# Another written-out order of all engines' steps for the first half of a fused attention and gated-MLP kernel

## The chip, the cores and the metric

The kernel runs on one core of a Trainium2 chip. The core has a matrix engine (PE, with its weight loads shown apart as PEld), a vector engine (DVE), a scalar engine (ACT), a general engine (POOL) and a queue that issues the transfers from and to HBM (SP). Each works through its own queue of instructions strictly in the order in which they were written, and waits at an instruction until what it needs is there. The metric is the time of one execution on the device in microseconds (us); lower is better.

## What is computed

Eight batches of windowed attention with eight heads, 576 positions and 64 numbers per head, and behind it a gated MLP with a spatial gate over the 576 positions (the reference, cut):

```python
scores = scale * np.matmul(q, k.transpose(0, 1, 3, 2))          # q, k, v: (8, 8, 576, 64)
mask = (rel >= 0) & (rel < 128)
scores = np.where(mask, scores + bias[None], -1000000000.0)
attn = np.exp(scores - np.max(scores, axis=-1, keepdims=True))
attn = attn / (np.sum(attn, axis=-1, keepdims=True) + 1e-09)
x = np.matmul(attn, v)                                          # then (8, 576, 512)

h = gelu(x @ w_in)                                              # w_in: (512, 1024)
u, v = h[..., :512], h[..., 512:]
v_n = (v - mu) / np.sqrt(var + 1e-06) * g_ln
v_s = np.einsum('ts,bsd->btd', w_sg, v_n) + b_sg[None, :, None] # w_sg: (576, 576)
out = x + (u * v_s) @ w_out                                     # w_out: (512, 512)
```

## The kernel before

The work is cut into steps, each a closure that issues a few instructions on one engine. A step's name is a letter or two and a number. Attention goes by pairs of heads: 32 pairs, numbered 0 to 31, four to a batch. The MLP goes by batch, 0 to 7. All matrix products of the MLP are made of three products of high and low halves, so everything that goes into them is split into a high part (ACT) and a low part (POOL or DVE).

The steps of pair n (`Pair.STEPS`), in the order of their needs:

- SP: q loads query and key, L loads the values (six transfers).
- PE: a and c are the scores of the first and second half of the positions for pairs 0 to 4; * is both at once for the later pairs.
- DVE: A, B, C, G add the bias and find the maxima of four score banks (lines 273 and 266). ACT: e, E, f, F, j are the exponentials. DVE: R inverts the sums (lines 294 and 295). POOL: r, s, S scale.
- PE: z, t, T transpose; DVE: X, Y copy the transposed weights out under a mask (line 318); ACT: P copies the first block.
- PE: 2 and v (for later pairs 3 and V) multiply with the values (lines 329 and 342). ACT: x gathers the result (lines 350 and 351), h takes its high part (line 356), POOL: l its low part (line 359), ACT: k a copy of the last columns (line 362).

The weights are split at the start, a tile k at a time: SP i loads; ACT d; DVE m, b, o (lines 183, 185, 187); POOL +; ACT H; then the low part -, on POOL for even k and on DVE for odd k (line 194). Tiles 0 to 7 are w_in, of which 4 to 7 are needed by u, and 8 to 11 are w_out. The spatial weights go by wl, wH, w- (SP, ACT, POOL); tl, tH, t- and bl, bH, b- are their tail and the bias; gb loads the gain. The loads of all these share a ring of four buffers, so a load waits until the step that last read its buffer is done: w-, + and so on.

The steps of batch b's MLP:

- PE: v, per block of 128 positions (in batch 0 in four parts, w and v); ACT: vg; DVE: nv..b and nv..c, POOL: nv..p, ACT: nv..h, DVE: vn normalize it.
- The same for the last 64 positions: PE tt; DVE tj; ACT tg; DVE nt..b and nt..c (lines 579 to 587); POOL nt..p; ACT nt..h; DVE tn (line 595, into vA).
- PE: u, eight sums to a batch (lines 559 to 561 with `xs` first); ACT: uc, ug.
- PE: y, eight spatial sums (the same lines with `ws`), whose last two matmuls alone read what tn wrote; DVE gm, ACT gh, POOL gl gate and split.
- PE: O, the output sums (Oa is the first three quarters of the first one); DVE oa adds, SP D stores.

A step y020 is batch 0, column block 2, half 0; nv30b is block 3 of batch 0.

What sets the order is a string, `ORDER`, with all step names. A small planner checks that each step comes after what it needs and that buffers are free, and runs the steps in that order. A manual dependency then keeps each engine's instructions in the order of the string. So the string is each engine's queue; steps of different engines that stand side by side in it need not run side by side.

```python
for run in plan.run(ORDER.split()):
    before = len(nc.cur_bb.bb.instructions)
    run()
    for i in nc.cur_bb.bb.instructions[before:]:
        if i.engine in last:
            tc.add_manual_dep(i, last[i.engine], ...)
        last[i.engine] = i.name
```

Of the kernel before, what the change touches and what calls it, by code (L numbers as in the profile page):

```python
# [21 lines left out]
def attention_gmlp(  # L22
# [754 lines left out]
    for b in range(B):  # L777
# [7 lines left out]
        T2 l1 q5 d6 G3 z2 +4 Y2 a4 F3 L3 P2 j3 -2 A4 22 v2 k1 H4 m6 e4 R3 -4 B4 i3 w21 x2 o5 c4 b6 h2 L5 r3 w11 j4 s3 C4
        w31 E4 G4 S3 t3 f4 w01 X3 F4 l2 i10 T3 d3 z3 Y3 +5 w12 q6 P3 k2 R4 *5 o6 H5 m3 i11 -5 b3 w22 A5 s4 q7 w32 +6 e5
        B5 23 w02 v3 j5 o3 i8 C5 S4 E5 H6 G5 +3 L4 x3 f5 r4 t4 -6 h3 T4 X4 d11 l3 i9 z4 Y4 H3 d8 -3 m11 k3 v03 P4 m8 F5
        b11 24 v01 b8 R5 v4 o11 vg03 o8 vg01 s5 nv30b v02 x4 r5 v00 nv30c nv10b nv30p t5 z5 S5 d9 X5 +11 nv30h T5 P5 +8
        d10 Y5 nv10p H11 35 m10 H8 V5 vn03 -11 vg00 nv10c u000 nv00b -8 L6 x5 nv10h b10 *6 vn01 nv00c vg02 L7 o10 u001 A6
        +10 nv20b u010 nv00p uc00 B6 q8 nv20p nv00h nv20c H10 u011 vn00 nv20h bl m9 C6 -10 tt0 uc01 G6 vn02 u020 bH b9  # L790
        tj0 u021 o9 tg0 b- u030 nt0b +9 uc02 nt0c H9 u031 nt0p -9 nt0h *7 uc03 tn0 ug0 y000 q9 A7 B7 h5 y020 h4 l5 C7 G7
        y001 l4 j6 k5 F6 y021 k4 E6 gm00 f6 e6 y010 gm02 E7 R6 s6 j7 y011 gh00 S6 f7 gh02 gl00 y030 gm01 e7 gh01 r6 gl02
        F7 z6 t6 y031 P6 X6 gl01 R7 T6 s7 gm03 Oa0 Y6 gh03 S7 gl03 *8 r7 O02 q10 A8 e8 B8 E8 C8 O00 j8 G8 f8 36 z7 oa00
        t7 V6 P7 oa02 F8 D00 D02 R8 s8 T7 L9 x6 X7 O03 S8 h6 Y7 l6 r8 37 k6 oa03 V7 D03 O01 L8 x7 h7 l7 *9 oa01 k7 D01
# [10 lines left out]
        S14 oa10 v23 Y13 r14 D10 vg22 nv22b t14 vg23 nv22c u230 x12 nv22p nv32b nv22h 313 nv32c V13 vn22 nv32p u231 L15
        x13 X14 nv32h *15 uc23 vn23 ug2 L14 y210 A15 h13 B15 h12 z14 l13 y220 q17 P14 C15 l12 G15 k13 T14 y211 Y14 e15
        E15 *16 gm21 F15 f15 y200 gh21 q19 A16 j15 gl21 B16 e16 y221 E16 C16 R15 f16 G16 y201 s15 gm22 F16 S15 gh22 t15
        gm20 j16 y230 gl22 gh20 R16 k12 gl20 314 y231 r16 s16 V14 gm23 S16 gh23 r15 Oa2 gl23 x14 X15 h14 l14 T15 O23 Y15
        k14 z15 t16 oa23 P15 O20 D23 315 T16 oa20 V15 D20 O21 L16 x15 X16 h15 Y16 l15 L17 *17 oa21 k15 u300 A17 q18 e17
        B17 v30 j17 C17 D21 f17 G17 E17 z16 u301 F17 P16 R17 v31 uc30 s17 S17 vg30 r17 nv03b t17 vg31 316 tt3 nv03c nv13b  # L810
        nv03p V16 nv03h nv13c vn30 u330 nv13p L19 x16 X17 nv13h z17 u331 vn31 P17 tj3 *19 uc33 tg3 nt3b O22 q21 A19 nt3p
        B19 nt3c e19 v32 C19 nt3h oa22 G19 D22 f19 tn3 j19 v33 E19 F19 R19 u320 r19 s19 vg32 vg33 nv23b T17 S19 u310
        nv33b nv23p nv33c u321 Y17 nv33p nv33h u311 nv23c uc32 vn33 nv23h *18 uc31 vn32 h16 ug3 l16 y320 q20 A18 B18 k16
        y300 C18 e18 G18 y321 E18 f18 j18 y301 gm32 F18 gh32 R18 y330 gl32 gm30 gh30 s18 317 y310 S18 gl30 t19 y311 r18
        z19 y331 gm31 P19 gh31 gl31 V17 gm33 gh33 Oa3 gl33 L18 x17 X19 h17 l17 T19 O32 Y19 k17 z18 t18 oa32 P18 319 O30
        D32 V19 oa30 D30 T18 L20 x19 X18 O33 h19 Y18 l19 k19 318 oa33 V18 D33 O31 L21 x18 h18 l18 *20 oa31 k18 D31 u400
        A20 e20 B20 tt4 j20 C20 f20 G20 u401 tj4 E20 F20 *21 uc40 R20 s20 u430 q22 A21 r20 tg4 S20 B21 t20 q23 v40 C21
        e21 nt4b E21 j21 nt4c u431 f21 G21 nt4p nt4h X20 T20 v41 F21 tn4 uc43 Y20 R21 v42 vg40 r21 s21 vg41 nv04b S21
        nv14b nv04p v43 nv14c nv04c nv14p nv04h nv14h vn40 z20 u420 vn41 vg42 P20 vg43 nv24b *22 nv34b nv24p nv34c u410
        q24 A22 nv34p nv34h u421 B22 C22 u411 e22 nv24c j22 G22 f22 z21 320 t21 vn43 V20 nv24h uc42 vn42 E22 y400 F22 L23  # L820
        X21 P21 x20 R22 T21 s22 h20 y401 Y21 uc41 r22 S22 *23 l20 ug4 y420 q25 A23 k20 gm40 B23 t22 gh40 y410 gl40 C23
        G23 e23 321 y421 E23 j23 z22 f23 V21 gm42 F23 P22 gh42 R23 y430 L22 X22 x21 s23 h21 S23 T22 y411 Y22 r23 l21 *24
        gl42 gm41 k21 gh41 y431 gl41 q27 A24 e24 B24 Oa4 E24 C24 gm43 f24 G24 gh43 322 z23 t23 F24 V22 gl43 P23 j24 R24
        T23 x22 X23 O43 r24 s24 h22 Y23 S24 l22 323 O40 oa43 V23 k22 D43 oa40 D40 O41 L24 x23 h23 l23 L25 *25 oa41 k23
# [53 lines left out]
```

## Time and profile before

| | us |
|---|---|
| median of 3 runs | 641.43 |
| the runs | 641.43, 639.53, 645.07 |
| profiled execution, first to last instruction (its span) | 639.6 |
| PE busy, share of the span | 606.7, 95% |
| DVE busy | 385.3, 60% |
| ACT busy | 356.2, 56% |
| POOL busy | 236.7, 37% |

The profile comes from one execution; it has the span, and of the whole time of that execution nothing beyond it, so the median of the runs stands beside it: 641.43 to 639.6. Busy is the time in which an engine executes. A row with min/median/max gives the length of one instruction in ns. In the rows in order of time the first two numbers are start and length in us, and a bracket at the end tells how long the engine was idle before and who ended that.

### The profile page before, as it was taken

The page shows a single profiled execution, that of the slowest core. Times are in us where ns is not written, and L with a number is a line of the kernel's source. Part 1 is how long each engine was busy: PE and PEld are TensorE (multiplying, and loading weights), DVE is VectorE, ACT ScalarE, POOL GpSimd, SP SyncE. Part 2 cuts the span into 40 slices and gives each one's busy share as a digit, 9 for nine tenths or more (in the row PEclk, how much of TensorE's full clock was granted, in tenths as well). Part 3 has the DMA queues.
Part 4 walks back from the last instruction along what each step waited for, and adds up shares of the span by engine and source line. Part 5 has one row for each costly group of instructions (what it writes and reads, how often), then busy time and mean ns, then how long its engine had stood idle before and what let it go on. Part 6 is the DMA issues. An engine that isn't in the chain of part 4 may idle for free.

```text
span 639.6 us, 14817 instructions
## 1 busy us (share of the span) xinstructions
PE 606.7 (95%) x5664; PEld 552.6 (86%) x5664; DVE 385.3 (60%) x1297; ACT 356.2 (56%) x1045; POOL 236.7 (37%) x237
## 2 busy tenths in 40 slices
PE   4877789999999999999999999999999999999997
PEld 2555579898999898998999989998999989999896
DVE  5899788445854587545753577547664465452611
ACT  8784756645582676725672478647483455543430
POOL 4776633632244323632233142542235222441220
PEclk9999699999999999999999999999999999999999
DMA  8875331051132413223311512224122321110001
GB/s 277 261 214 180 107 116 38 1 172 57 40 114 70 141 38 104 71 78 98 93 38 58 173 38 76 79 95 115 40 93 73 103 94 40 40 39 38 0 1 75
DMA packets 55931, 57.24 MB, mean 89 GB/s; under 512 B 8498, under 2 KB 45362, under 8 KB 55860
## 3 DMA queue, kind: packets, MB, share of 16 engines
q1 hardware_dynamic: 55860, 56.28, 28.3%
q8 instruction: 45, 0.74, 0.5%
q14 instruction: 26, 0.21, 0.1%
HBM read 46.83 MB, written 9.44 MB: 88 GB/s over the span
## 4 chain that ended last, share of the span: by engine, by line
PE 84%; DVE 8%; ACT 2%; issue 2%; POOL 1%; DMA 1%; SPq 0%; POOLq 0%; DVEq 0%
PE ps_m L559 20%; PE ps_m L561 19%; PE ps_m L560 19%; PE ps_s L342 7%; PE ps_s L247 4%; PE ps_a L309 4%; PE ps_a L247 3%; DVE e L266 2%; DVE px L318 2%; PE ps_a L342 1%; PE ps_m L707 1%; PE ps_m L706 1%; DVE tmp L187 1%; PE ps_m L643 1%; PE ps_m L645 1%
## 5 line engine op out<-in xcount | busy, mean ns | idle before, releaser
L282 ACT ACTIVATE e<-e,stats 128x128 f32<-128x128 f32 (+1 forms) x320 | 121.1, 380 | 33.8 <-DVE stats L266 32.5
L299 POOL TENSOR_TENSOR e<-e,rr 128x512 f32<-128x512 f32 (+1 forms) x96 | 79.9, 853 | 130.4 <-DVE rr L295 103.0
L559 PE MATMUL ps_m<-ws,vn 128*128 128x288 f32 x256 | 79.1, 309 | 0.0
L559 PE MATMUL ps_m<-g,wo 128*128 128x288 f32 x256 | 78.8, 308 | 0.0
L559 PE MATMUL ps_m<-xs,wi 128*128 128x288 f32 x256 | 78.4, 306 | 0.1
L561 PE MATMUL ps_m<-g,wo 128*128 128x288 f32 x256 | 75.9, 296 | 0.0
L561 PE MATMUL ps_m<-xs,wi 128*128 128x288 f32 x256 | 75.7, 296 | 0.0
L561 PE MATMUL ps_m<-ws,vn 128*128 128x288 f32 x256 | 75.7, 296 | 0.0
L560 PE MATMUL ps_m<-xs,wi 128*128 128x288 f32 x256 | 75.6, 295 | 0.0
L560 PE MATMUL ps_m<-ws,vn 128*128 128x288 f32 x256 | 75.6, 295 | 0.0
L560 PE MATMUL ps_m<-g,wo 128*128 128x288 f32 x256 | 75.0, 293 | 0.5 <-POOL g L719 0.5
L359 POOL TENSOR_TENSOR xs<-xf,xs 128x576 fp32r<-128x576 f32 x32 | 45.8, 1432 | 77.8 <-ACT xs L356 77.6
L318 DVE TENSOR_TENSOR px<-ps_a,m_old 128x512 f32<-128x512 f32 x64 | 43.9, 687 | 49.5 <-PE ps_a L309 37.0
L584 POOL TENSOR_TENSOR rs<-rs,mhalf 128x1 f32<-128x1 f32 (+1 forms) x40 | 32.6, 814 | 96.7 <-DVE rs L581 90.1
L719 POOL TENSOR_TENSOR g<-u,g 128x576 fp32r<-128x576 f32 x32 | 45.5, 1423 | 52.3 <-ACT g L716 52.2
L282 ACT ACTIVATION_READ_ACCUMULATOR e<-e,stats 128x1 f32 (+1 forms) x320 | 60.1, 188 | 0.0
L742 DVE TENSOR_TENSOR xf<-ps_m,xf 128x576 f32<-128x576 f32 x32 | 24.1, 757 | 58.4 <-PE ps_m L561 58.4
L712 DVE TENSOR_TENSOR u<-ps_m,u 128x576 f32<-128x576 f32 x32 | 24.2, 755 | 51.2 <-PE ps_m L707 51.2
L559 PE MATMUL ps_m<-wi,xs 128*128 128x512 f32 x128 | 53.7, 419 | 0.5 <-ACT wi L192 0.5
L247 PE MATMUL ps_s<-qk 64*64 64x192 f32 (+2 forms) x632 | 42.5, 351 | 11.3 <-DMA qk<-qkT 7.3
L559 PEld LDWEIGHTS ps_m<-xs,wi 128*128 128x128 f32 x256 | 48.3, 189 | 4.1 <-issue 1.9
L561 PE MATMUL ps_m<-wi,xs 128*128 128x512 f32 x128 | 51.2, 400 | 0.7 <-POOL xs L359 0.7
(122 smaller groups left out, 1538.5 us busy)
## 6 DMA issues: line engine op xcount, KB each, us to landing
qk<-qkT SPq DMA_DIRECT2D x32, 576.0 KB, 3.9
vt<-v_in SPq DMA_DIRECT2D x64, 256.0 KB, 3.4
outT<-xf SPq DMA_DIRECT2D x32, 288.0 KB, 2.1
wst<-w_in SPq DMA_DIRECT2D x8, 512.0 KB, 4.5
vt<-v_in SPq DMA_DIRECT2D x64, 32.0 KB, 2.9
wst<-w_out SPq DMA_DIRECT2D x4, 512.0 KB, 4.6
wst<-w_sgT SPq DMA_DIRECT2D x4, 288.0 KB, 5.9
vd<-v_in SPq DMA_DIRECT2D x64, 16.0 KB, 2.6
```

The costliest lines, as they stand in the source:

```text
L247: return lambda: nc.tensor.matmul(dst, qk[js, 0, q0:q0 + R], qk[js, 1, k0:k1], start=True, stop=True)
L282: nc.scalar.activation(x, x, AF.Exp, bias=self.nm[0:n, i:i + 1], scale=-1.0, accum_out=self.sm[0:n, i:i + 1])
L299: nc.gpsimd.tensor_tensor(x, x, self.rr[0:n, i:i + m].rearrange("p (m o) -> p m o", o=1).broadcast_to([n, m, c]), ALU.mult)
L309: burst([lambda t=t: nc.tensor.transpose(ct[:, t * P:(t + 1) * P], self.pr[j][:, t, :], ident) for t in range(T)])
L318: nc.vector.tensor_tensor(xv[:, :, :, i, :], cv, m.rearrange("p (t h c) -> p t h c", t=1, h=1).broadcast_to([P, T, 2, R]), ALU.mult)
L342: return lambda: nc.tensor.matmul(x1[heads[j], q0 + lo // 2 * R if t < 0 else q0 + t * R:q0 + (hi + 1) // 2 * R], block, px[j][:, (half * ...
L359: nc.gpsimd.tensor_tensor(lo_of(self.xs), self.xf, hi_of(self.xs).bitcast(F32), ALU.subtract)
L559: nc.tensor.matmul(dst, ah, bh, start=(first and i == 0), stop=False)
L560: nc.tensor.matmul(dst, ah, bl, start=False, stop=False)
L561: nc.tensor.matmul(dst, al, bh, start=False, stop=(last and i == n - 1))
L584: nc.gpsimd.tensor_tensor(x["rs"][0:rows], x["rs"][0:rows], mhalf[0:rows], ALU.pow)
L719: nc.gpsimd.tensor_tensor(st[f"g{f}"][:, 1, :], st["u"][:, f, :], st[f"g{f}"][:, 0, :].bitcast(F32), ALU.subtract)
```

## The change

The string `ORDER` is replaced by another one. The names in it are the same, so no step is added, removed or given to another engine; the steps stand otherwise as far as u400, the first sum of batch 4, and are word for word the same from u400 to the end, on all five engines. The table of names tells a reader little; its first line before and now:

```diff
-        i0 q0 i7 d0 wl2 m0 a0 b0 i1 o0 A0 d7 +0 q1 B0 wH2 H0 m7 c0 L1 w-2 d1 C0 -0 G0 e0 b7 wl0 a1 m1 j0 o7 q2 b1 E0 A1
+        i0 q0 wl2 q1 i1 i7 d0 m0 b0 o0 +0 a0 A0 B0 c0 wl0 d7 d1 wH2 e0 E0 j0 m1 m7 b1 o1 b7 C0 G0 +1 w-2 wl3 gb q2 i4 L0 H0
```

The queue of SP at its start, before (`qk` is a load q, `wst` a weight load, `vt` and `vd` a load L):

```order
L168 DMA wst_153<-w_in 128x512
L221 DMA qk_155<-qkT 128x1152
L168 DMA wst_157<-w_in 128x512
L168 DMA wst_161<-w_sgT 128x576
L168 DMA wst_181<-w_in 128x512
L221 DMA qk_191<-qkT 128x1152
L229 DMA vt_210<-v_in 128x4x128
```

and now:

```order
L168 DMA wst_153<-w_in 128x512
L221 DMA qk_155<-qkT 128x1152
L168 DMA wst_157<-w_sgT 128x576
L221 DMA qk_159<-qkT 128x1152
L168 DMA wst_161<-w_in 128x512
L168 DMA wst_163<-w_in 128x512
L168 DMA wst_205<-w_sgT 128x576
L168 DMA wst_231<-w_sgT 128x576
L550 DMA gb_147<-g_ln 128x512
L221 DMA qk_234<-qkT 128x1152
```

The load i7 moved from third to sixth place, the load L1 moved back behind all of these, and two spatial weights and the gain went ahead of the third load of queries and keys.

DVE's queue around tn0 (line 595 into `vA`), before; ahead of it stand bias, norm and low-part steps, behind it step A of pair 7 (bias 6):

```order
L542 SCALAR_TENSOR_TENSOR wsB_145<-wsh_1195,bsel_149,wst_1160 2x576
L579 BN_STATS st_1230<-vg_1198 64x6
L580 BN_AGGR mv_1231<-st_1230 64x2
L581 TENSOR_SCALAR rs_1232<-mv_1231 64x1
L587 SCALAR_TENSOR_TENSOR vg_1198<-vg_1198,mv_1231,gb_147 64x512
L194 TENSOR_TENSOR wo_142<-tmp_975,wo_142 128x512
L595 SCALAR_TENSOR_TENSOR vA_1254<-vg_1198,rs_1232,vA_1254 64x512
L273 COPY_PREDICATED ps_a_1259<-sel_94,ps_a_1259 128x2x64
L266 ISA e_1257,stats1_137<-ps_a_1259,bias6_118 128x128
```

and now:

```order
L587 SCALAR_TENSOR_TENSOR vg_1117<-vg_1117,mv_1169,gb_147 64x512
L194 TENSOR_TENSOR wo_142<-tmp_997,wo_142 128x512
L542 SCALAR_TENSOR_TENSOR wsB_145<-wsh_1141,bsel_149,wst_1023 2x576
L185 TENSOR_SCALAR tmp_1135<-tmp_1135 128x512
L185 TENSOR_SCALAR tmp_1036<-tmp_1036 128x512
L595 SCALAR_TENSOR_TENSOR vA_1180<-vg_1117,rs_1170,vA_1180 64x512
L187 SCALAR_TENSOR_TENSOR tmp_1135<-wst_1021,tmp_1135 128x512
L273 COPY_PREDICATED ps_a_1205<-sel_94,ps_a_1205 128x2x64
L266 ISA e_1203,stats0_135<-ps_a_1205,bias4_114 128x128
```

The steps A, B, C, G of pair 6 (bias 4 and 5) moved from ahead of tn0 to behind it, with o9, o8 and -9.

PE's queue around V5 (line 342 into `ps_s`), before; the sums u of batch 0 (`xs,wi`) begin behind it:

```order
L309 MATMUL ps_a<-ident,e 128x128 x4
L322 MATMUL ps_a<-ident,e_1_133 128x128
L309 MATMUL ps_a<-ident,e 128x128 x4
L329 MATMUL ps_s<-p_2_130,vd_128 128x64
L342 MATMUL ps_s<-px,vt 64x64 x2
L342 MATMUL ps_s<-px,vt 64x128 x12
L342 MATMUL ps_s<-px,vt 64x64 x4
L559 MATMUL ps_m<-xs,wi 128x288
```

and now:

```order
L561 MATMUL ps_m<-xs,wi 128x288
L329 MATMUL ps_s<-p_2_130,vd_128 128x64
L342 MATMUL ps_s<-px,vt 64x64 x2
L342 MATMUL ps_s<-px,vt 64x128 x12
L342 MATMUL ps_s<-px,vt 64x64 x4
L559 MATMUL ps_m<-xs,wi 128x288
```

Seven of the eight sums u and the tail tt0 moved ahead of V5; u021 and the scores *6 stand between V5 and the first spatial sum. At the end of the changed part, on ACT, the steps h and k of pairs 16 to 19 moved together, each h with the k behind it that waits for POOL's l, behind x18, the last gather ahead of u400.

More of the change, by code (lines that the diff above doesn't have):

```diff
@@ L785, in attention_gmlp @@
[L785 to L794, printed above, removed]
@@ L805, in attention_gmlp @@
[L805 to L814, printed above, removed]
@@ L815, in attention_gmlp @@
[L815 to L824, printed above, removed]
@@ new lines, in attention_gmlp @@
+        w31 w10 Y3 +5 l2 -2 *5 w11 o3 +3 E4 tH H4 R4 t- s4 S4 A5 B5 w21 23 w32 v3 C5 k2 H3 j5 G5 -7 -3 f5 H5 x3 h3 e5 E5 k0
+        l3 F5 -6 r4 -4 w01 t4 T4 w22 v03 v02 w12 X4 Y4 R5 -5 vg03 nv30b nv30c v01 z4 r5 nv30p P4 k1 vg01 24 v4 w02 v00 nv10b
+        d10 nv30h vn03 x4 s5 z5 t5 k3 vg02 nv10p nv10c S5 q6 i11 u000 nv20b nv10h vn01 nv20c m10 u001 vg00 d11 b10 o10 +10
+        i8 L5 q8 L7 i9 bl nv00b nv20p nv00p uc00 d8 P5 X5 nv00c m11 H10 u010 u011 uc01 nv20h T5 tt0 nv00h vn02 b11 vn00 o11
@@ new lines, in attention_gmlp @@
+        u030 u031 tj0 u020 +11 d9 H11 tg0 -10 bH Y5 35 V5 m8 nt0b nt0p m9 nt0c x5 nt0h uc03 -11 b- b9 b8 tn0 u021 uc02 ug0
+        *6 q7 L6 o9 +9 A6 B6 o8 y020 y021 y010 y011 +8 C6 gm02 G6 e6 H8 H9 -9 -8 f6 j6 F6 E6 gm01 gh01 gh02 R6 *7 A7 B7 C7
+        y000 r6 s6 gl02 z6 y001 G7 gm00 P6 h5 f7 gh00 E7 j7 e7 t6 X6 F7 S6 T6 y030 y031 Y6 gm03 R7 gh03 *8 A8 B8 C8 G8 gl00
+        gl01 Oa0 s7 r7 gl03 S7 z7 t7 O00 P7 36 T7 V6 O03 x6 h6 X7 Y7 37 V7 j8 oa00 oa03 q9 E8 h4 l4 k4 x7 F8 h7 l6 f8 e8 R8
+        l5 l7 r8 O02 *9 oa02 A9 B9 C9 G9 k5 f9 k6 e9 F9 j9 E9 R9 O01 v10 vg10 oa01 v11 s9 vg11 t9 nv01b nv11b X9 q11 L8 D03
@@ new lines, in attention_gmlp @@
+        y311 ug3 j18 q20 L19 L18 D22 D20 gm31 gh31 y301 gm30 E18 gh30 x17 R18 y320 z19 P19 y321 gm32 gl31 s19 S19 t19 X19
+        r18 T19 Y19 s18 y330 y331 z18 gh32 gl32 gl30 S18 t18 319 V19 gm33 gh33 P18 T18 x19 X18 Oa3 Y18 gl33 318 O30 V18 O31
+        x18 *20 oa31 oa30 O33 oa33 D33 q21 L20 L21 O32 oa32 D32 h19 l19 k19 h18 l18 k18 h17 l17 k17 h16 l16 k16 D31 D30 u400
+        A20 e20 B20 tt4 j20 C20 f20 G20 u401 tj4 E20 F20 *21 uc40 R20 s20 u430 q22 A21 r20 tg4 S20 B21 t20 q23 v40 C21 e21
+        nt4b E21 j21 nt4c u431 f21 G21 nt4p nt4h X20 T20 v41 F21 tn4 uc43 Y20 R21 v42 vg40 r21 s21 vg41 nv04b S21 nv14b
@@ new lines, in attention_gmlp @@
+        nv04p v43 nv14c nv04c nv14p nv04h nv14h vn40 z20 u420 vn41 vg42 P20 vg43 nv24b *22 nv34b nv24p nv34c u410 q24 A22
+        nv34p nv34h u421 B22 C22 u411 e22 nv24c j22 G22 f22 z21 320 t21 vn43 V20 nv24h uc42 vn42 E22 y400 F22 L23 X21 P21
+        x20 R22 T21 s22 h20 y401 Y21 uc41 r22 S22 *23 l20 ug4 y420 q25 A23 k20 gm40 B23 t22 gh40 y410 gl40 C23 G23 e23 321
+        y421 E23 j23 z22 f23 V21 gm42 F23 P22 gh42 R23 y430 L22 X22 x21 s23 h21 S23 T22 y411 Y22 r23 l21 *24 gl42 gm41 k21
+        gh41 y431 gl41 q27 A24 e24 B24 Oa4 E24 C24 gm43 f24 G24 gh43 322 z23 t23 F24 V22 gl43 P23 j24 R24 T23 x22 X23 O43
@@ new lines, in attention_gmlp @@
+        r24 s24 h22 Y23 S24 l22 323 O40 oa43 V23 k22 D43 oa40 D40 O41 L24 x23 h23 l23 L25 *25 oa41 k23 tt5 A25 q26 e25 B25
+        t24 tj5 u500 E25 D41 j25 X24 v52 C25 tg5 G25 nt5b u501 f25 nt5c F25 T24 nt5p uc50 z24 v53 Y24 P24 nt5h R25 r25 tn5
+        u510 s25 S25 vg52 t25 324 vg53 nv25b V24 nv35b nv25p v50 nv25c L26 x24 nv35c nv25h X25 nv35p nv35h vn52 u511 vn53
+        vg50 nv05b v51 uc51 nv05c nv05p nv05h z25 u520 vg51 vn50 P25 nv15b u530 nv15c nv15p u521 nv15h vn51 u531 uc52 *27
+        h24 uc53 l24 ug5 O42 q28 A27 B27 k24 C27 e27 y500 G27 E27 oa42 j27 T25 D42 f27 y501 Y25 F27 R27 *26 gm50 s27 gh50
@@ new lines, in attention_gmlp @@
+        S27 y530 q29 A26 r27 gl50 e26 B26 y520 E26 C26 f26 G26 325 y531 F26 j26 V25 R26 gm53 r26 s26 gh53 y521 L27 x25 S26
+        h25 gl53 t26 gm52 y510 X26 gh52 l25 T26 gl52 y511 k25 Y26 z26 t27 gm51 P26 326 V26 gh51 gl51 T27 L29 x26 X27 O51 h26
+        Y27 l26 k26 z27 Oa5 oa51 P27 D51 *29 O52 A29 e29 B29 j29 C29 E29 327 G29 O50 f29 oa52 V27 F29 oa50 D52 D50 R29 O53
+        s29 L28 x27 h27 S29 l27 *28 oa53 r29 k27 D53 v62 q31 A28 e28 B28 q30 j28 C28 z29 v63 f28 G28 F28 E28 v60 P29 R28 r28
```

64 lines of the change are left out of this document (32 added, 32 removed).

## The prediction

> **What bounds the kernel now.** I read first the page's busy shares and slices, then a table of stretches of the span, then who ended PE's waits, then single steps in order of time.
>
> ```profile
> span 639.6 us, 14817 instructions
> PE 606.7 (95%) x5664; PEld 552.6 (86%) x5664; DVE 385.3 (60%) x1297; ACT 356.2 (56%) x1045; POOL 236.7 (37%) x237
> PE   4877789999999999999999999999999999999997
> ```
>
> PE is busy 95% of the span, and its slices are below nine tenths only at the start and at the last one. So I cut the span where the queues change character (columns: us, then busy time and count of PE, PEld, DVE, ACT, POOL, then granted clock, DMA share, GB/s):
>
> ```profile
> 7.40:28.00 20.60, 15.56 (x127) 10.62 (x129) 18.88 (x75) 15.91 (x56) 14.60 (x12) 1.00 0.96 305
> 28.00:66.90 38.90, 30.04 (x341) 23.50 (x337) 36.67 (x123) 25.59 (x100) 24.97 (x23) 0.96 0.63 199
> 66.90:106.50 39.60, 34.09 (x301) 28.86 (x300) 32.24 (x78) 23.03 (x48) 18.60 (x17) 0.87 0.27 78
> 106.50:124.00 17.50, 16.05 (x123) 15.82 (x122) 8.94 (x35) 14.94 (x52) 10.22 (x9) 1.00 0.09 33
> 124.00:362.50 238.50, 238.50 (x2338) 221.14 (x2336) 137.58 (x477) 129.12 (x382) 80.75 (x81) 1.00 0.29 86
> 362.50:639.60 277.10, 272.36 (x2448) 252.60 (x2444) 149.09 (x499) 141.38 (x393) 85.65 (x84) 1.00 0.20 63
> ```
>
> Two things are to be seen. From 124.0 to 362.5 PE has no gap at all: no order can gain there, it can only lose. And up to 106.5 DVE is the fuller engine (18.88 of 20.60, 36.67 of 38.90, 32.24 of 39.60), while PE has gaps of 5.0, 8.9 and 5.5 us. The longest single gaps of PE there end on DVE's step X or Y (line 318):
>
> ```profile
> PE ps_a L322 <- DVE px L318: 6.5, 3, 3.5
> ```
>
> **The change, part by part.** *From u400 on* (362.5 us) every queue is as it was, so the last 277.1 us stay; what the change is worth is the moment at which u400 starts. *Between the first sums y of batch 0 and u400* PE was gapless and its work is the same. So the anchor is the first sum y: y000 before, y020 now.
>
> ```profile
> 88.56 0.94 PE L247 MATMUL ps_a<-qk 64*64 64x64 f32 x22
> 90.14 0.40 PE L559 MATMUL ps_m<-xs,wi 128*128 128x288 f32 x1
> 105.20 0.40 PE L559 MATMUL ps_m<-ws,vn 128*128 128x288 f32 x1
> ```
>
> y000 begins at 105.20. PE's queue ahead of the first y holds the same steps before and now, but for the scores of pair 7 (*7), which come after four sums y now. Scores last 90.14 - 88.56 = 1.58 us. So no change means y020 at 105.20 - 1.58 = 103.6, and the gain is 103.6 less its new start.
>
> *DVE's queue to tn0*, the last step that a first y needs, is what sets that start. It has seven steps less in it now: o8, o9, -9 and A6, B6, C6, G6 come behind tn0.
>
> ```profile
> 91.55 0.29 DVE L273 COPY_PREDICATED ps_a<-sel,ps_a 128x128 f32<-128x128 uint8 x1
> 92.44 0.68 DVE L579 BATCH_NORM_STATS2 st<-vg 128x6 f32<-128x512 f32 x1
> 96.11 0.28 DVE L273 COPY_PREDICATED ps_s<-sel,ps_s 128x128 f32<-128x128 uint8 x1
> 96.85 0.29 DVE L273 COPY_PREDICATED ps_s<-sel,ps_s 128x128 f32<-128x128 uint8 x1
> L187 DVE SCALAR_TENSOR_TENSOR tmp<-wst,tmp x12: 630/686/3682, 8.3 to 100.1; 128x512 int32<-128x512 int32 x12
> L194 DVE TENSOR_TENSOR wi<-tmp,wi x4: 628/1176/1789, 19.3 to 70.8; 128x512 fp32r<-128x512 f32 x4
> ```
>
> A step A (91.55 to 92.44) is 0.89, B the same, C (96.11 to 96.85) 0.74, G the same, o and - at their fastest 0.63: 1.78 + 1.48 + 1.89 = 5.2 us. With every step at the median that it has in this trace, DVE's queue from m0 (7.4) through tn0 sums to 75.9 us before and 70.7 now. Before, it took 99.1 us (the first three stretches of the table): 23.2 us more than its steps. That extra is 4.4 in the first stretch (16.2 us of steps, through A2), 10.5 in the second (28.4, through G5), 8.3 in the third (31.3, through tn0). I put the same three stages on the new queue.
>
> Opening, through A2 (16.9 us of steps now: m4, b4, o4 are in, -7 is out). The load of q2 stood behind wl0 on SP and was issued at 12.89; now wl3, which waits for w-2 on POOL, and gb stand ahead of it, and i7 is the sixth load instead of the third, with d7 ahead of d1 on ACT.
>
> ```profile
> 12.89 0.35 SPq L221 DMA_DIRECT2D qk<-qkT x1
> 23.66 0.90 PE L247 MATMUL ps_s<-qk 64*64 64x64 f32 x4
> ```
>
> By POOL's three steps in a row I put q2 at about 17.5, 4.6 later. Its data is used by a2 only at 23.66, over 10 us after the old issue, so a2 is hardly moved; d7 ahead of d1 costs ACT and DVE more. I take A2's end 1.0 later, at 29.0 (bounds 27 and 33).
>
> Second stage, to G5: 26.5 us of steps (-7 and -5 stand behind G5 now). Of the extra of 10.5, 8.3 is stretch (36.67 busy less 28.4 of steps): DVE steps that run beside POOL's (o at up to 3.68 for 0.63, - at up to 1.79). POOL's work beside it is as dense as before, so I keep its share, 26.5/28.4 of 10.5 = 9.8: G5 ends at 65.3. Bounds are none of it and twice of it.
>
> Here the Trainium skill speaks against the change: GPSIMD Engine Reference, section Key points, says that GpSimd shares its SBUF interfaces with VectorE and contends with DVE instructions of two SBUF inputs or in a two-port mode. The row of line 187 agrees (0.63 to 3.68). By the rule, what is packed tighter on both engines stretches more, up to the doubling (9.8 us more in the sum); by the rows it stretches as before.
>
> Third stage, to tn0: 27.3 us of steps. Of the old extra of 8.3, four waits make 6.6:
>
> ```profile
> 68.37 0.69 DVE L318 TENSOR_TENSOR px<-ps_a,m_old 128x512 f32<-128x512 f32 x1 [1.51 <-PE ps_a L309]
> 81.63 0.69 DVE L318 TENSOR_TENSOR px<-ps_a,m_old 128x512 f32<-128x512 f32 x1 [3.70 <-PE ps_a L309]
> 83.73 0.69 DVE L318 TENSOR_TENSOR px<-ps_a,m_old 128x512 f32<-128x512 f32 x1 [0.81 <-PE ps_a L309]
> 105.69 0.74 DVE L595 SCALAR_TENSOR_TENSOR vA<-vg,rs,vA 64x512 fp32r<-64x512 f32 x1 [0.60 <-ACT vA L592]
> ```
>
> X5 (81.63) waited 3.70 for t5, which stood on PE behind v4, v02 and v00. Now X5 comes after the norm steps nv..b, nv..c and vn of three tiles, so t5 is long done. I take 1.5 of waits and 1.7 of stretch: 3.2 (bounds 0 and 8.3). tn0 ends at 65.3 + 27.3 + 3.2 = 95.8.
>
> PE's side: between V5 and the first y stand u021 and *6. V5 needs Y5, which on DVE is 6.5 us of steps ahead of tn0's end: 89.3.
>
> ```profile
> 96.88 0.29 PE L559 MATMUL ps_m<-xs,wi 128*128 128x288 f32 x1
> 98.47 0.30 PE L559 MATMUL ps_m<-xs,wi 128*128 128x288 f32 x1
> 350.05 1.88 PE L342 MATMUL ps_s<-px,vt 128*64 128x64 f32 x36
> ```
>
> V5 1.9, u021 98.47 - 96.88 = 1.6, *6 1.6: y020 starts at 89.3 + 5.1 = 94.4, and its last two matmuls, which alone read tn0's result, find it there. Gain at the anchor: 103.6 - 94.4 = 9.2 us. PE reaches V5 early: u000 may start when -5 is done, 4.7 us of steps behind G5, about 70.5; seven sums u at 1.6, tt0 at 1.9 and T5 at 0.4 (13.5 us) later PE stands before V5 at 84. So the order turns several gaps into one of 3 to 5 us. What such gaps did to the clock:
>
> ```profile
> 44.69 0.30 PE L322 MATMUL ps_a<-ident,e 128*128 128x128 f32 x1 [3.45 <-DVE px L318]
> 46.00:49.40 3.40, 3.40 (x35) 0.50 0.18 74
> 63.97 0.41 PE L329 MATMUL ps_a<-p,vd 128*128 128x64 f32 x2 [2.65 <-issue]
> 69.90:80.10 10.20, 8.80 (x48) 0.50 0.28 82
> ```
>
> A gap of 3.45 was followed by 3.4 us at clock 0.50, one of 2.65 with smaller ones behind it by 10.2 us. In the half-clock stretch PE's work takes twice as long, and now nothing hides that: 1.7 us lost in the short one, 5.1 in the long one. I charge the short one: 9.2 - 1.7 = 7.5 us.
>
> *The join at u400.* On ACT and POOL h, l and k of pairs 19, 18, 17, 16 form one chain behind x18, which waits for V18:
>
> ```profile
> L350 ACT COPY xf<-ps_s x27: 582/587/596, 86.9 to 577.9; 128x512 f32<-128x512 f32 x27
> L351 ACT COPY xf<-ps_s x27: 213/218/245, 87.4 to 578.4; 128x64 f32<-128x64 f32 x27
> L356 ACT CAST xs<-xf x32: 656/674/682, 30.6 to 578.7; 128x576 fp32r<-128x576 f32 x32
> L359 POOL TENSOR_TENSOR xs<-xf,xs x32: 1407/1427/1673, 31.3 to 579.4; 128x576 fp32r<-128x576 f32 x32
> L362 ACT CAST xs<-xs x32: 223/245/254, 39.7 to 580.9; 128x64 fp32r<-128x64 f32 x32
> 345.13 0.38 PE L559 MATMUL ps_m<-g,wo 128*128 128x288 f32 x1
> 348.39 0.27 PE L322 MATMUL ps_a<-ident,e 128*128 128x128 f32 x1
> ```
>
> x18 0.8, then h 0.67 + l 1.43 + k 0.25 for each pair but the last k: 0.8 + 9.2 = 10.0. Over it lie O31, O33, O32 (348.39 - 345.13 = 3.2 each) and *20 (1.6): 11.2. It is hidden with 1.2 us to spare; if ACT or POOL come late by more, PE waits for l16. I charge nothing, bounds 0 and 2.
>
> The sum: 639.6 - 7.5 = 632.1 of span. The median of the runs shown, 641.4, lies 1.8 above the profiled span; kept on top: **634 us**.
>
> **Rivals.** *Clock:* the wait before V5 brings the long half-clock stretch of 10.2 us, 5.1 lost instead of 1.7; gain 9.2 - 5.1 = 4.1, so 637. For it: each of the two longest gaps was followed by such a stretch. Against: the gap may come out shorter. The Trainium skill, TensorE: Matmul & The Clock Gate, section HAM oscillation — how this bites in real kernels, says that no PE idle gap should exceed some 3.4 us, since the half clock comes back then; the trace agrees for the gap of 3.45 and shows the half clock behind 2.65 too.
>
> *New gaps where there were none:* between 124 and 362 the new queue groups pairs and sums otherwise; ten waits of 0.5 to 1 us (the size of the waits at 83.73 and 105.69) take 5 to 10 us; gain 0, about 641. Against: in these 238.5 us DVE is busy for 137.58, ACT for 129.12 and POOL for 80.75, and the old list had no wait with that.
>
> *Slower: DVE beside POOL.* If the stretch in the second stage, where POOL now has l1, +5, l2, -2, +3, t-, s4, S4, l3, -6 and r4 back to back, grows from 9.8 to 24 us (five steps o at 3.68 instead of 0.63 are 15), the gain of 7.5 becomes a loss of 6.7: 648. It decides from 17.3 on. Against: of the 23.2 us extra only 11.9 was stretch (DVE busy for 87.8 in the three stretches, 75.9 of it steps).
>
> **How the numbers follow.** About 1%, 6.4 us, is what a measurement of this kernel can tell from no change: faster means below 635.0. Forecast, gain 4 to 13: 0.58 (0.46 of it below 635.0, since the stage bounds lie about evenly around 7.5 to 8.5). Stretch much smaller, gain over 13: 0.07. Clock: 0.12, within 1%. New gaps: 0.11, within 1%. DVE slower: 0.12 (0.09 over 1%). So faster 0.53, same 0.38, slower 0.09. The range 627 to 643 holds the forecast, the clock and the gap rivals and a little of the last: 0.8.
>
> **What would show it.** Right: y020 starts at 92 to 97; tn0 ends near 95.8; X5 without a wait over 1 us; a gap of PE before line 342 of pair 5; no gap of PE from there to u400; u400 at 355. Wrong: y020 after 100, a DVE second stage of over 45 us, or gaps of PE between 115 and u400 that sum to over 3 us.

## The result and the profile after

| | before | after |
|---|---|---|
| median of the runs beside each other | 640.48 us (4 runs) | 633.75 us (4 runs, 633.17 to 635.48) |
| ratio | | 0.9894, 95% interval 0.9864 to 0.9925 |
| span of the profiled execution | 639.6 us | 633.8 us |
| time of the profiled execution | 641.43 us | 635.48 us |

The kernel became faster by 1.1% (0.8 to 1.4%). The prediction said 634.0 us. The profiled execution after is the slowest of its four, so the spans lie closer together (5.8 us) than the medians (6.7 us). The changed kernel was measured once more beside the experiments: 635.74 us against 640.73, ratio 0.9918 (0.9895 to 0.9942).

The page of the changed kernel: its span, its busy shares, TensorE's (PE's) slices, and the granted clock of the slices in tenths.

```profile
span 633.8 us, 14834 instructions
PE 603.6 (95%) x5664; PEld 550.9 (87%) x5664; DVE 374.3 (59%) x1297; ACT 355.4 (56%) x1047; POOL 232.7 (37%) x237
PE   2687999989999999999999999999999999999997
PEclk9878999999999999999999999999999999999999
```

The count of matmuls is what it was. PE's first two slices are emptier than before (the first five read 26879 instead of 48777), and from the fifth on they are full but for the ninth and the last. The table of stretches of the changed kernel, with the columns of the one in the prediction, says by how much:

```profile
7.40:28.00 20.60, 11.39 (x113) 7.83 (x113) 14.11 (x64) 12.24 (x43) 11.07 (x9) 1.00 0.67 214
28.00:66.90 38.90, 32.55 (x343) 25.25 (x344) 31.64 (x133) 29.43 (x110) 25.81 (x23) 0.83 0.75 232
66.90:106.50 39.60, 39.18 (x367) 35.27 (x367) 34.99 (x94) 31.32 (x75) 20.48 (x21) 1.00 0.33 94
106.50:124.00 17.50, 17.50 (x185) 16.79 (x185) 11.21 (x48) 8.38 (x33) 8.67 (x8) 1.00 0.26 81
124.00:362.50 238.50, 236.38 (x2266) 218.16 (x2268) 135.50 (x472) 130.30 (x397) 79.02 (x79) 0.99 0.26 79
362.50:633.80 271.30, 266.52 (x2404) 247.47 (x2394) 145.04 (x475) 137.58 (x375) 85.72 (x84) 1.00 0.22 68
```

PE's idle time, the first number less the second, went from 5.0 to 9.2 us in the first stretch, from 8.9 to 6.4 in the second, from 5.5 to 0.4 in the third, from 1.5 to 0 in the fourth, and from 0 to 2.1 in the fifth. So the change pays at the opening, gains in the next three stretches, and pays once more later. The clock column needs care: the clock's records begin only at 24.5 us in this trace (28.9 before, up to 37.9 in the runs below), and ahead of them the view shows 1.00, while PE's rows there are as long as at half clock. Step 20's 36 matmuls, ahead of the first record (37.8 us) in the run of experiment 5, and at full clock in that of experiment 7:

```profile
30.00 3.47 PE L342 MATMUL ps_a<-px,vt 128*64 128x64 f32 x36
```
```profile
27.64 1.88 PE L342 MATMUL ps_a<-px,vt 128*64 128x64 f32 x36
```

Who ended PE's waits after (us in total, times, longest) names the places:

```profile
PE ps_s L247 <- issue: 4.8, 1, 4.8
PE ps_a L329 <- DMA vd<-v_in: 2.8, 1, 2.8
PE ps_m L559 <- ACT vg L633: 2.1, 1, 2.1
PE ps_a L247 <- DVE px L318: 2.1, 1, 2.1
```

The first two are the opening (a1, and step 20, which needs the last data of L0). The third is new, far behind the opening: v11. The fourth is *5, the scores of pair 5, which wait for Y3. In order of time, PE's rows at *5, the first matmul of u000, of V5, of the first sum y (y020) and of v11, and the first one of u400, where both orders are the same again:

```profile
58.51 1.21 PE L247 MATMUL ps_a<-qk 64*64 64x64 f32 x15 [2.11 <-DVE px L318]
...
76.75 0.40 PE L559 MATMUL ps_m<-xs,wi 128*128 128x288 f32 x1
...
90.59 0.66 PE L342 MATMUL ps_s<-px,vt 128*64 128x64 f32 x10
...
95.77 0.40 PE L559 MATMUL ps_m<-ws,vn 128*128 128x288 f32 x1
...
140.24 0.58 PE L559 MATMUL ps_m<-wi,xs 128*128 128x512 f32 x1 [2.12 <-ACT vg L633]
...
356.85 0.29 PE L559 MATMUL ps_m<-xs,wi 128*128 128x288 f32 x1
```

The first y starts at 95.77, which is 7.85 us earlier than the 103.62 that mean no change. u400 starts at 356.85 instead of 362.55, so 5.7 us are left there, and the rest of the kernel is as long as it was: 276.9 us against 277.1 to the end of the span. Between the first y and u400, 2.1 us were given back: 3.9 at v11, as the first experiment shows, less 1.8 that the old order lost behind its first sums (1.45 of it is the idle time of the fourth stretch before).

The 7.85 us at the first y have two parts. From its first matmul (7.3 us) to the first y PE was idle for 16.0 us instead of 19.4, which is 3.4 of them. The other 4.4 are the same matmuls in less time: PE was busy for 72.5 us instead of 76.9 (without *7). Of these busy times 21.4 us were at half clock or ahead of the first clock record, instead of 28.8.

### The profile page after: what moved, and what is told of

The parts are those of the page before. It is cut to its first block, busy times and chain, and to the rows that moved or that the text cites. A ratio compares the mean times of both kernels' runs of the same rounds, so it can differ in the third digit from the quotient of the medians.

```text
span 633.8 us, 14834 instructions
## 1 busy us (share of the span) xinstructions
PE 603.6 (95%) x5664; PEld 550.9 (87%) x5664; DVE 374.3 (59%) x1297; ACT 355.4 (56%) x1047; POOL 232.7 (37%) x237
## 4 chain that ended last, share of the span: by engine, by line
PE 85%; DVE 4%; ACT 2%; issue 1%; POOL 0%; POOLq 0%; DVEq 0%
PE ps_m L559 21%; PE ps_m L561 20%; PE ps_m L560 20%; PE ps_s L342 8%; PE ps_a L309 4%; PE ps_a L247 4%; PE ps_s L247 3%; ACT e L282 1%; PE ps_m L707 1%; PE ps_m L706 1%; PE ps_m L643 1%; PE ps_m L645 1%; PE ps_s L329 1%; DVE px L318 1%; DVE e L266 1%
## 5 line engine op out<-in xcount | busy, mean ns | idle before, releaser
L282 ACT ACTIVATE e<-e,stats 128x128 f32<-128x128 f32 (+1 forms) x320 | 121.2, 381 | 39.4 <-DVE stats L266 38.4
```

Source lines behind the costliest of these rows:

```text
L282: nc.scalar.activation(x, x, AF.Exp, bias=self.nm[0:n, i:i + 1], scale=-1.0, accum_out=self.sm[0:n, i:i + 1])
```

## What the runs were to tell apart

My theory after the result, S: VectorE (DVE) sets the pace only up to Y3, at 58 us; from there to v11 PE's own queue does, without a gap over 0.3 us, and the last sums' preparation on DVE (tn0) has time to spare. On its side stand two prices that the change pays by the way, one at d7's place in the opening, one at v11. The rival, D, is the step of the prediction: DVE's queue all the way to tn0 sets the first y. A second rival: the new order of the middle, from 106 to 357 us, has a part in the gain.

All ten kernels ran against the kernel before; what was made together ran on the same chip.

| run | median us | ratio to before, 95% interval | first y | u400 |
|---|---|---|---|---|
| before | 640.5 to 641.1 | | 105.20 (y000) | 362.55 |
| after | 633.75 | 0.9894 (0.9864 to 0.9925) | 95.77 | 356.85 |
| vg10 behind v11 | 632.35 | 0.9853 (0.9826 to 0.9879) | 96.82 | 353.96 |
| d7, m7, b7 later | 631.31 | 0.9842 (0.9817 to 0.9867) | 91.77 | 352.85 |
| new start alone | 635.42 | 0.9905 (0.9874 to 0.9936) | 95.73 | 357.52 |
| new middle alone | 647.36 | 1.0103 (1.0079 to 1.0126) | (old start) | 371.15 |
| after, again | 635.74 | 0.9918 (0.9895 to 0.9942) | 95.35 | 356.42 |
| more PE work | 638.00 | 0.9947 (0.9928 to 0.9967) | 100.40 | 359.93 |
| more DVE work at b- | 635.03 | 0.9911 (0.9889 to 0.9933) | 95.16 | 356.11 |
| both edits | 627.65 | 0.9792 (0.9764 to 0.9820) | 89.86 | 347.00 |
| more DVE work at Y3 | 637.39 | 0.9946 (0.9929 to 0.9963) | 97.28 | 358.32 |
| both edits, opening anew | 628.54 | 0.9815 (0.9792 to 0.9838) | 92.77 | 349.90 |

## Experiment 1: the wait at v11

v10 and v11 write the two halves of one PSUM tile (pv0); vg10 is the ScalarE (ACT) step that reads v10's half. The new list writes vg10 between them. The order of the list is also the order in which reads and writes of a tile are known, so v11's first matmul was made to wait for vg10, though their halves differ. The old list has vg10 behind v11. The edit moves one word; no engine's queue changes, only the wait goes:

```diff
- ... R9 O01 v10 vg10 oa01 v11 s9 vg11 ...
+ ... R9 O01 v10 oa01 v11 vg10 s9 vg11 ...
```

> The new order with one name moved: vg10 stands behind v11 in the string instead of ahead of it. No engine's queue changes; only the wait of v11's first matmul for vg10 is gone, which the writing order brought in because both use the same PSUM tile. Theory (this wait opens the 2.12 us gap before v11 and the half clock behind it that makes v11 4.60 us long instead of 2.80): gap and slow stretch both go, 3.9 us less than the new order, about 630. Rival (PE would wait there anyway, for something else of the same moment, or the gap moves on to the next step): no change, 633 to 634.

In the changed kernel, ACT at that place (the first of the ten exponentials of pair 9, the end of the last one, and then vg10):

```profile
134.27 0.40 ACT L282 ACTIVATE e<-e,stats 128x128 f32<-128x128 f32 x1 [3.50 <-DVE stats L266]
...
138.09 0.19 ACT L282 ACTIVATION_READ_ACCUMULATOR e<-e,stats 128x1 f32 x1
138.30 1.28 ACT L633 ACT_TABLE_LOAD   x1
139.59 0.60 ACT L633 ACTIVATE vg<-ps_m 128x512 f32<-128x512 f32 x1
```

vg10 stands behind the exponentials and a table load of 1.28 us, and ends at 140.19; v11 begins at 140.24. With the edit the last matmul of v10 and the first of v11 follow each other, and vg10 and vg11 come after both:

```profile
138.77 0.39 PE L561 MATMUL ps_m<-wi,xs 128*128 128x512 f32 x1
139.00 0.40 PE L559 MATMUL ps_m<-wi,xs 128*128 128x512 f32 x1
```
```profile
142.00 1.09 ACT L633 ACTIVATE vg<-ps_m 128x512 f32<-128x512 f32 x2 [1.37 <-PE ps_m L561]
```

From v10 to u400 it takes 217.75 us instead of 221.68: 3.9 less, as expected. That is more than the gap of 2.12, since in the changed kernel PE ran at half clock right behind it (the granted clock is the third number from the end):

```profile
140.50:143.90 3.40, 3.40 (x9) 2.63 (x9) 0.75 (x3) 0.00 (x0) 1.79 (x2) 0.50 0.72 230
```

In it a matmul of v11 begins 0.43 us behind the one before (141.05, 141.48 and so on); at full clock that is 0.23 (138.77 to 139.00). Two of the later runs had the gap of 2.12 without the half clock, and needed 220.1 us from v10 to u400. So the wait costs 2.4 us, and the half clock behind it, where it comes, 1.5 more. The first y came 1.05 us later in this profile, in which the half clock of the opening lasted to 42.3 us instead of 38.1, so that the profiled execution shows 2.9 of the 3.9.

## Experiment 2: d7 in the opening

d7, m7 and b7 are the first steps of input weight 7. The new list has d7 ahead of d1 on ACT, where i7 is now the sixth load. The edit puts the three behind the first pair's exponentials:

```diff
- ... c0 wl0 d7 d1 wH2 e0 E0 j0 m1 m7 b1 o1 b7 C0 G0 +1 ... f0 F0 H1 a1 R0 o7 ...
+ ... c0 wl0 d1 wH2 e0 E0 j0 m1 b1 o1 C0 G0 +1 ... f0 F0 d7 H1 a1 R0 m7 b7 o7 ...
```

> The new order with d7, m7 and b7 moved behind the first pair's exponentials and R0, so that d1 no longer stands behind d7 on the scalar engine while d7 waits for the sixth load. Theory (the late opening of the new order, A2 ending at 31.8 instead of 28.0, comes from d7's wait and is passed on to the first sum y): a1 and A1 start about 3 us earlier, y020 2 to 3 us earlier, 631 to 632. Rival (the opening is made up for before the first y, or the loads L0 and i4 bind it): A1 earlier but y020 within 0.7 us of 95.8, time unchanged at 633 to 634.

In the changed kernel, first on ACT, where line 179 is step d, then on DVE:

```profile
12.11 0.66 ACT L179 ACTIVATE wst<-wst 128x512 int32<-128x512 uint32 x1 [4.72 <-DMA wst<-w_in]
```
```profile
14.43 0.76 DVE L183 TENSOR_SCALAR tmp<-tmp 128x512 f32<-128x512 f32 x2 [3.46 <-ACT tmp L181]
```

ACT stands 4.72 us before d7, because i7's data is not there, while d1, e0 and wH2 wait behind it; DVE stands 3.46 before m1, and C0 and G0 are behind that. With the edit, the same places:

```profile
10.97 0.67 ACT L179 ACTIVATE wst<-wst 128x512 int32<-128x512 uint32 x1 [3.60 <-DMA wst<-w_in]
```
```profile
14.69 2.52 PE L247 MATMUL ps_s<-qk 64*64 64x64 f32 x24 [2.01 <-issue]
...
27.83 0.45 PE L329 MATMUL ps_a<-p,vd 128*128 128x64 f32 x2
```

a1 starts at 14.69 instead of 17.44, step 20 at 27.83 instead of 29.31 and without a wait for vd. The second follows from SP's queue: wH2, earlier on ACT, lets w-2 on POOL and with it wl3 go earlier, and the loads of pair 0's values stand behind wl3. These two rows are the first and the last load of L0 in the changed kernel, then with the edit:

```profile
19.86 0.42 SPq L229 DMA_DIRECT2D vt<-v_in  x1
...
23.64 1.24 SPq L232 DMA_DIRECT2D vd<-v_in  x2
```
```profile
17.09 0.43 SPq L229 DMA_DIRECT2D vt<-v_in  x1
...
20.43 1.24 SPq L232 DMA_DIRECT2D vd<-v_in  x2
```

Y3's end moved from 58.36 to 54.44, the first y from 95.77 to 91.77, u400 from 356.85 to 352.85: 3.9 to 4.0 us at all three, so that what the opening loses is paid in full at the end. That is more than the 2 to 3 us expected, and the clock has a part in it: without the wait for vd the half clock, over at 27.89, does not come back, and step 20's 36 matmuls take 1.88 us; in the changed kernel it comes back at 27.87 for 10.2 us, and they take 3.47. So 1.6 of the 3.9 us arise in step 20, by the clock.

## Experiments 3 and 4: the new start alone, the new middle alone

Here the list is cut in two; the place where the two orders meet is called the seam. The first kernel follows the new list up to v10 and then does what is left in the old list's order; the second follows the old one up to u100 and then the new.

> The new order up to v10 (all of batch 0), and from there the remaining steps in the order of before. Theory (all gain is made ahead of batch 1, and the new order of batches 1 to 3 only costs the gap at v11): 9 us under before, 631 to 632, no gap of PE behind 124 us. Rival (the new order of batches 1 to 3 brings part of the gain): 635 or more.

The first y stands where it did (95.73), and the interval of the time's ratio covers the 0.9894 of the changed kernel. But the time missed the 631 to 632 us of the theory and lies in the rival's range (635 or more), and there is a gap of PE behind 124 us, which the theory had excluded. The seam brought it:

```profile
139.36 0.50 PE L559 MATMUL ps_m<-wi,xs 128*128 128x512 f32 x1 [2.48 <-DVE xf L742]
```

PE's work from the first y to u400 is the same in both orders. It took 261.8 us here and 257.1 with the new middle without its wait at v11 (experiment 1): 4.7 more. Of these, 2.5 are the wait at the seam, and 1.65 the half clock behind it, since v10 took 4.45 us instead of 2.80. So, but for the seam, the old middle is as fast as the new one to within 0.5 us. That rests on these rows of one execution; the median alone would speak for the rival.

> The order of before up to u100 (all of batch 0), and from there the remaining steps in the new order. Theory (the new order of batches 1 to 3 brings nothing and has the wait of v11 for vg10): 2 to 4 us over before, 643 to 644, with the gaps of the start as before. Rival (the middle gains): under 640.

```profile
153.40 0.79 PE L559 MATMUL ps_m<-wi,xs 128*128 128x512 f32 x1 [4.74 <-ACT vg L633]
```

The new middle alone made the kernel slower than before, by 1.0% (0.8 to 1.3%). The wait at v11 grew to 4.74 us, with 6.8 us of half clock behind it, because ACT's exponentials came later against PE here: the first one starts 2.0 us behind v10, in the changed kernel 0.9 ahead of it. In this profile, the slowest of six executions (649.83 us), u400 is 8.6 later: 1.3 were lost before the first y, where there are 17.1 us at half clock, some 4.7 are the wait and 2.7 the half clock behind it. In the medians the loss is 6.3 us, more than the 2 to 4 expected. The second rival falls by both runs: the middle has no part in the gain, and all of it is made before the first sums y.

## Experiments 5 and 6: more work on PE, more work on DVE

The changed kernel again, then u021 done four times over (line 683), then b- done four times over (line 542). Neither changes a result.

```diff
+ for _ in range(4 if (b, f, i) == (0, 2, 1) else 1):
      mm3(st[f"pu{f}"][:, i, 0:S2], ...)
```
```diff
+ for _ in range(4):
      nc.vector.scalar_tensor_tensor(out=wsB[R:R + 2], ...)
```

> The changed kernel itself once more, so that the next three stand beside it on one chip: 633.8 us in the profiled execution, 633 to 636 us in the median; first y at 95.8, fourth MLP matmul u400 at 356.9, a gap of 2.1 us before v11 with TensorE at half clock behind it.

> u021's twelve matmuls are done four times instead of once: 36 more matmuls, about 4.8 us of TensorE work between V5 and the first y and not one instruction more on any other engine (the tile holds the same sums at the end). Theory P (after the change TensorE's own full queue sets the first y; VectorE's tn0 was done 0.6 us before the first y began and some 2.4 us before the matmul that reads it): the first y and everything behind it come about 4.8 us later, time +4 to +5.5 us against the changed kernel of the same chip. Theory D (my prediction: VectorE's queue down to tn0 sets the first y and TensorE has 3 to 5 us to spare ahead of it): the work lies in that spare time, +0 to +1.8 us.

> b- (0.81 us on VectorE, seven VectorE instructions ahead of the end of tn0) is done four times instead of once: about 2.4 us more of VectorE work ahead of tn0, and nothing more on any other engine. Theory D: tn0 and with it the first y come 2.4 us later, time +2 to +2.8 us. Theory P: tn0 ends at about 97.6, where the matmul that reads it is due, so that the first y moves by 0 to 0.5 us, and the time by 0 to +0.5 us.

With 4.7 us more on PE (u021 lasts 6.58 instead of 1.84) the first y came 5.05 us later than in the repeated kernel, 100.40 against 95.35. That is theory S; with the spare time of theory D it would have been hidden. At the end 3.5 us are left in the profiles and 2.3 in the medians, less than the 4 to 5.5 that I expected. 1.5 of it is seen: the half clock at v11, there in the repeated kernel's profile, is not there in this one. Among executions of one granted clock the difference is as expected: at 0.996 the five of this kernel have a median of 638.3 us, the two of the changed kernel 633.3 and 633.6.

With 2.5 us more on DVE, tn0 ended at 97.07 instead of 94.74, and the first y began at 95.16. In that profile, the last matmul of y020 that does not need tn0, and the first that does (vA); then tn0's last step on DVE:

```profile
96.74 0.29 PE L562 MATMUL ps_m<-ws,vn 128*128 128x288 f32 x1
97.13 0.40 PE L707 MATMUL ps_m<-wsA,vA 128*128 128x288 f32 x1
```
```profile
96.33 0.74 DVE L596 SCALAR_TENSOR_TENSOR vA<-vg,rs,vA 64x512 fp32r<-64x512 f32 x1
```

A matmul adds 0.13 to 0.14 there, so the one that reads vA was due at 96.88 and came at 97.13: 0.25 late for 2.5 us of work put ahead of it. So tn0 had some 2.3 us to spare, and D falls. The work is not free all the same: behind the first y, z6 and T6 wait 0.31 and 0.35 for pair 6's later softmax, and from the first y to v10 it takes 40.8 us instead of 39.4. The median is 0.7 below the repeated kernel's; the intervals of the ratios cover each other, and the 2.0 to 2.8 us of theory D are not there.

## Experiment 7: both edits together

> The two edits that each beat the changed kernel, together: vg10 written behind v11, and d7, m7 and b7 behind the first pair's exponentials. If they act in different places and neither feeds on the other's gain, the gains add: 4.0 us at the first y and 3.9 us at v11, so u400 at about 349 us and a profiled execution of about 626 us, a median of 626 to 629 us. If the clock takes one of them back, u400 stands at 351 to 353 and the time at 629 to 631 us.

627.65 us, ratio 0.9792 (0.9764 to 0.9820): 8.1 below the changed kernel of the same chip, with 4.0 and 3.9 expected. This version beats both kernels, by 2.1% and 1.3%. PE from 106.5 to u400's old place has no gap at all:

```profile
106.50:124.00 17.50, 17.50 (x205) 16.66 (x205) 8.09 (x33) 8.60 (x34) 9.61 (x9) 1.00 0.33 105
124.00:362.50 238.50, 238.50 (x2276) 220.01 (x2275) 142.25 (x505) 135.67 (x409) 77.60 (x80) 1.00 0.28 85
```

The profiled execution, with 623.9 us of span, is the fastest of the four, and it has no half clock from its first clock record (26.1 us) to the tail. So u400 at 347.0 is 2 us better than the 349 expected, and the median is the fairer number.

## Experiment 8: more work on DVE at Y3

About as much DVE work as at b- (2.9 us, there 2.5), put ahead of *5 instead of ahead of tn0:

```diff
- for i, m in enumerate((m_old, m_own)):
+ for i, m in ([(0, m_old)] + [(1, m_own)] * (5 if self.n == 3 and j == 1 else 1)):
```

> The second of Y3's two VectorE instructions is done five times instead of once: four more instructions of 0.6 us each, 2.4 us more of VectorE work, as much as three repeats of b- made, but at 58 us of the span instead of 93. Theory S (VectorE's queue sets the pace only up to Y3, for which TensorE waits 2.1 us in the scores of pair 5; from there to the first y TensorE's own queue does): the wait of TensorE for Y3 grows from 2.1 to about 4.5 us, the first y comes 2.4 us later (97.8 instead of 95.4 to 95.8), u400 too, and the time is 2 to 3 us over the changed kernel's 633.8 to 635.7. Rival D (the wait at pair 5 is local and later waits absorb it, or TensorE's queue alone counts from the opening on): the first y moves by 0 to 0.5 us and the time by as little.

DVE, then PE, in that profile:

```profile
56.53 3.58 DVE L318 TENSOR_TENSOR px<-ps_a,m_own 128x512 f32<-128x512 f32 x5
```
```profile
60.26 1.24 PE L247 MATMUL ps_a<-qk 64*64 64x64 f32 x15 [5.02 <-DVE px L318]
```

PE's wait grew from 2.11 to 5.02. Y3 began 1.2 us earlier than in the changed kernel, so that it ended 1.75 later (60.11), and the first y came 1.5 later (97.28), u400 1.5 as well. The size is smaller than the 2.4 expected by what the opening of this execution was ahead; its half clock ended at 32.5 us instead of 38.1. From Y3's end on it goes one for one, and the rival named here, that later waits absorb it, does not hold. The medians agree, though more weakly: the ratio is 0.9946 (0.9929 to 0.9963) against 0.9894 and 0.9918 of the changed kernel, and the interval of the second one (0.9895 to 0.9942) meets it.

Over all profiles with the new start, this is the time from Y3's end to the first y: 37.2 to 37.4 us in seven of them, with 3.1 to 3.4 us of half clock in *5 and behind it; 36.0 in the two without that half clock; 42.0 with the 4.7 us of extra matmuls. Y3's end itself lies between 53.8 and 60.1. So one number and Y3's end give the first y.

## Experiment 9: the opening written once more

Both edits, and on top of them e0 ahead of d1, C0 and G0 ahead of m1, and m7, b7, o7 behind B1:

```diff
- ... c0 wl0 d1 wH2 e0 E0 j0 m1 b1 o1 C0 G0 +1 ... a1 R0 m7 b7 o7 A1 B1 ...
+ ... c0 wl0 e0 d1 wH2 E0 j0 C0 G0 m1 b1 o1 +1 ... a1 R0 A1 B1 m7 b7 o7 ...
```

> The kernel with both edits, and the opening written anew once more: e0 ahead of d1 on ScalarE, C0 and G0 ahead of m1, and A1 and B1 ahead of m7, b7 and o7 on VectorE. If each us of TensorE's waits in the opening is still worth one us at the end (TensorE waits 2.1 us for a1 and 2.1 for c1 there, and the first of these waits for C0 behind m1, b1 and o1): a1 1.2 us earlier, c1 3 us earlier, A2 2 to 3 us earlier, the first y at 87 to 88 instead of 89.9, time 624 to 626 us. If the first y is held by something else by now (the later loads, VectorE beside GpSimd): first y at 89 to 90 and the time at 627 to 628 us as with both edits alone.

A miss: a1 came 1.1 us earlier, as expected, but A2 ended at 31.27 instead of 30.05, and the first y came at 92.77 instead of 89.86. PE's waits in that opening:

```profile
13.72 2.52 PE L247 MATMUL ps_s<-qk 64*64 64x64 f32 x24 [0.97 <-PE ps_s L247]
19.74 1.11 PE L309 MATMUL ps_a<-ident,e 128*128 128x128 f32 x4 [3.50 <-POOL e L299]
...
28.63 0.66 PE L329 MATMUL ps_a<-p,vd 128*128 128x64 f32 x2 [1.51 <-DMA vd<-v_in]
```

Behind a1, t0 waits 3.50 us for s0 on POOL, instead of 1.51, and vd is late again. +1 stands ahead of both s0 and w-2 on POOL and needs o1, which is behind C0 and G0 now: +1 and w-2 start 1.9 us later than with both edits alone, and the load of vd is issued 2.1 later. No run tries this by itself. The clock has a part here too: half clock lasted to 32.2 us instead of 26.1, and step 20's 36 matmuls took 3.31 us instead of 1.88, so 1.4 of the 2.9 us at the first y arise there, by the clock. The waits' places changed, their sum did not fall, and the time, 628.54 us, is no better than with both edits alone.

## Why the prediction came out right, step by step

**Where it can gain.** Right. From u400 on, both kernels take the same time, and what is won is won before the first sums y: the new start alone has all of it, the new middle alone loses.

**What sets the first y.** This is the step that failed: "DVE's queue to tn0, the last step that a first y needs, is what sets that start". DVE's queue sets it only up to Y3. From there PE has 36.0 us of its own work to the first y, 37.4 with the half clock behind *5, and not one gap over 0.3 us. tn0 was ready at 95.15, near the forecast 95.8, but 2.3 us before it was read. The seven steps taken off DVE's queue did shorten it, but PE did not stand waiting for tn0. An estimate from experiment 6: had they stayed, their 5.2 us less the 2.3 to spare would have made tn0 some 2.9 us late. No run puts them back, and none separates the new order of PE's steps from that of DVE's; which of the moved steps brings how much stays open.

**PE's side.** Wrong, and this hid the first error. I let u000 start when -5 is done, at 70.5, and got a gap of 3 to 5 us before V5. -5 ended at 72.42, and u000 started at 76.75 because sixteen steps of PE's own queue, from v3 to t5, stood between G5's end and it, which I had not added up. So there is no gap before V5. Had I added PE's queue from *5 to y020, its 36 us would have stood beside DVE's sum. The two sums end near each other here (94.4 by DVE's queue in the forecast, 95.8 by PE's in the trace), so the first y's start alone does not tell the right one from the wrong one; experiments 5, 6 and 8 do. Nor does the forecast's sum have the other half of the gain, the 4.4 us that the same matmuls took less.

**Opening.** A2 at 29.0, bounds 27 to 33; it ended at 31.83. I had looked for q2 behind wl3, whose data is needed late, and not for L0, which stands behind q2 on the same queue and whose vd PE waited 2.78 us for. I had priced both together with d7 ahead of d1 at 1.0; the stage took 7.5 us more than its 16.9 of steps, where 4.7 was forecast, and experiment 2 shows 4.0 at the first y for the place of d7, m7 and b7.

**DVE beside POOL.** The share that I kept, 9.8 us extra in the second stage, was too large by 4: from A2's end to G5's end at 64.13 it took 32.3 us, 5.8 more than the 26.5 of steps. In the second stretch DVE was busy for 31.64 us (36.67 before), with POOL as busy as before (25.81 against 24.97). The longest step o there took 2.28 us (3.68 before). So the rule of the Trainium skill that I had set against the change (GPSIMD Engine Reference, Key points) did not decide it. The error at the opening, 2.8, and this one, 4.0, go against each other; the third stage had 3.7 us extra, where 3.2 was forecast.

**The clock.** 1.7 us charged before V5. That half clock did not come, but a stretch of 3.4 us came behind *5 and cost 1.4 (37.4 less 36.0), and one behind v11 cost 1.5. The half clock in the opening seems to cost as well: in the seven profiles with the changed kernel's opening it ended between 32.5 us (experiment 8) and 42.3 (experiment 1), and Y3's second instruction (in experiment 8 the first of the five) ended between 57.2 and 59.6, in nearly the same order: 2.4 us later for 9.8 us more of it. The prediction's reading of the rows before is wrong in one place: the 10.2 us from 69.9 on came behind 1.8 us of smaller gaps between 66.45 and 69.87, not behind the gap of 2.65, which had ended 5.9 us earlier (the last section has the count).

**No new gap up to u400.** Wrong by one: v11, 2.12 us of wait and 3.9 in all. It is the mechanism of the rival "new gaps", at one place in place of ten, and it does not come from the grouping of pairs and sums, but from where vg10 is written. The order of each queue cannot show it; the waits that an instruction carries can.

**The join at u400.** Right, there is no wait there.

**The sum.** 7.5 us forecast, 5.8 in the profiles, 6.7 in the medians. At the first y 9.2 was forecast and 7.85 came. The 1.7 charged for the clock ahead of V5 did not come there; 2.15 were lost behind the first y instead. Of the signs that were to show the forecast right, X5 without a wait and tn0 near 95.8 came; the gap ahead of V5 did not, and v11 brought one that was not to be. That 634.0 stands 0.25 us from the measured 633.75, with the wrong engine named for the first y, is luck: the errors go against each other. What the prediction had right is where the gain is made, and its direction.
